# Attention loaded four heads at a time with scores in 32-row tiles, and the second layer of two token runs as seven block products

## The chip, the cores and the metric

One core of one Trainium2 chip. The metric is the device time of one execution in microseconds; the time before is the median of three runs, 688.4 us (688.04 to 689.31). Nothing else runs on the chip.

## What is computed

```python
# attention, for 4 batches x 12 heads x 448 positions x 64 dimensions
scores = np.matmul(q, k.transpose(0, 1, 3, 2)) / np.sqrt(64)
scores = cap * np.tanh(scores / cap)
attn = np.exp(scores - np.max(scores, axis=-1, keepdims=True))
attn = attn / (np.sum(attn, axis=-1, keepdims=True) + 1e-09)
x = np.matmul(attn, v)            # then as 1792 tokens x 768
# multilayer perceptron
h = x @ w_in                      # 768 x 2048, handed in as 64-bit floats
out = np.maximum(0.01 * h, h) @ w_out     # 2048 x 768
```

## The kernel before, in words

**Order of the work.** The program is written as steps (`plan.add`): a rank, the engines that may do it with a cost on each, what it reads and writes, and which old tiles must be free. `Plan.issue` runs a list scheduler over these costs, and emits the instructions in the order that it finds; each engine's order, and which engine a step goes to, are fixed then. The table `T` at the top holds rank offsets of each kind of step, which shift that order.

**Attention.** The 48 heads are 24 pairs (`plan_pair`, line 435). `load_qk` (415) reads the keys or queries of a pair in four transfers of 32 of a head's 64 floats per row; VectorE transposes them in blocks of 32 (line 448), so that a pair lies with its two heads in the upper and lower 64 partitions. Scores are made in four groups of keys: three wide ones of 128 keys for each head as two tiles of 64 rows (499, or 493 where operands are split), and a last one with the 64 keys left of both heads as a block diagonal of 128 rows (496, 490). The first 12 pairs use plain 32-bit matmuls, which show as two records each; later pairs split each operand into a rounded part and a remainder and add three products. ScalarE takes tanh (521) and exp (523) of each group. The groups take turns on two score tiles of two PSUM banks each, `sc`. Values (504) are four groups of two matmuls with 64 columns each, into one of two banks `po`. The sums of the exponentials over keys are added by groups (527, 528, 530) and then, for the first 12 pairs, summed over partitions by a matmul with ones (508) into the other bank `po`, copied and transposed (562). For later pairs (`late_of`, from `tv`) VectorE transposes and reduces them (546, 547) and a small matmul with `fold` (551) adds the parts. A reciprocal, a transpose and a product (581) give the scaled output.

**Layers.** Tokens are cut into four runs: 256, 512, 512 and 512. Run 0 converts each block of weights from 64-bit floats (622 to 629, ScalarE and VectorE), uses it and writes it to a scratch in memory. Run 1 (`plan_unit`, 647) loads these blocks again. From run 1 on every operand is split (`split`, 401: a cast on ScalarE, line 258, and a subtraction on VectorE or GpSimd, line 265) and multiplied as three products of 512 columns. Runs 0 and 1 accumulate in the two banks `m`.

**The last two runs** share their first layer: 2 x 2 blocks of tokens and weights, seven products instead of eight (`plan_blocks`, `plan_duo`, 847; matmuls at 895). Each of the 8 duos leaves four hidden blocks `C` (11, 12, 21, 22; two blocks of hidden features by two runs). `plan_hidden` (950) splits each, and `plan_last` (962) makes the second layer from 18 units of weights (five or six blocks of 128 x 128 each): for each output block and each run 16 blocks x 3 matmuls at line 992, in steps of up to six; then a transpose (1005) and a store (634) in four transfers of 32 columns. The last store is shared by two queues.

## Time and profile before

| | us |
|---|---|
| median of 3 runs | 688.4 |
| profiled execution | 689.4 |
| its span, first to last instruction | 687.6 |
| TensorE busy | 653.6 (95%) |
| VectorE busy | 446.9 (65%) |
| ScalarE busy | 367.7 (53%) |
| GpSimd busy | 73.5 (11%) |
| mean granted TensorE clock | 0.99 |

A stretch's busy time of an engine is the time in which at least one of its instructions ran. A matmul's record lasts longer than the distance to the next, since matmuls are pipelined; the time that one costs is read from how many end in an unbroken stretch. Line 258 and line 265 are helpers that all casts, copies and subtractions share, so their groups are told apart by tile and shape. DMA share is the mean busy share of 16 DMA engines. The clock is given as a share of full speed, 2.4 GHz; the only other level is 1.2 GHz.

### The profile page before, as it was taken

The page shows a single profiled execution, that of the slowest core. Times are in us where ns is not written, and L with a number is a line of the kernel's source. Part 1 is how long each engine was busy: PE and PEld are TensorE (multiplying, and loading weights), DVE is VectorE, ACT ScalarE, POOL GpSimd, SP SyncE. Part 2 cuts the span into 40 slices and gives each one's busy share as a digit, 9 for nine tenths or more (in the row PEclk, how much of TensorE's full clock was granted, in tenths as well). Part 3 has the DMA queues.
Part 4 walks back from the last instruction along what each step waited for, and adds up shares of the span by engine and source line. Part 5 has one row for each costly group of instructions (what it writes and reads, how often), then busy time and mean ns, then how long its engine had stood idle before and what let it go on. Part 6 is the DMA issues. An engine that isn't in the chain of part 4 may idle for free.

```text
span 687.6 us, 8588 instructions
## 1 busy us (share of the span) xinstructions
PE 653.6 (95%) x2932; PEld 457.7 (67%) x2932; DVE 446.9 (65%) x693; ACT 367.7 (53%) x611; POOL 73.5 (11%) x87
## 2 busy tenths in 40 slices
...
GB/s 135 138 237 166 260 246 197 303 256 259 232 130 227 229 170 198 115 46 85 74 91 91 58 95 86 84 47 23 82 33 57 91 42 73 38 92 92 38 27 33
DMA packets 186308, 85.60 MB, mean 124 GB/s; under 512 B 148240, under 2 KB 172816, under 8 KB 186256
## 3 DMA queue, kind: packets, MB, share of 16 engines
...
q0 software_dynamic: 768, 1.38, 1.1%
...
q8 instruction: 25, 0.41, 0.3%
q14 instruction: 27, 0.22, 0.1%
HBM read 66.85 MB, written 18.09 MB: 124 GB/s over the span
## 4 chain that ended last, share of the span: by engine, by line
PE 77%; DVE 8%; ACT 6%; DMA 6%; issue 1%; SPq 1%; DVEq 0%; ACTq 0%
PE m L673 27%; PE sc L992 19%; PE sc L895 11%; PE po L504 7%; PE po L895 4%; PE sc L493 3%; DMA bank<-in_moe_w_in_dram 3%; PE m L895 2%; ACT exps L521 2%; PE sc L499 2%; DVE bank L626 1%; DVE ws L629 1%; ACT exps L523 1%; PE sc L490 1%; DMA scratch<-ws 1%
## 5 line engine op out<-in xcount | busy, mean ns | idle before, releaser
L258 ACT CAST w<-ws 128x384 fp32r<-128x384 f32 (+2 forms) x99 | 62.9, 654 | 133.8 <-PE sc L992 75.1
L265 DVE TENSOR_TENSOR w<-ws,w 128x384 fp32r<-128x384 f32 (+2 forms) x93 | 68.0, 744 | 74.8 <-ACT w L258 74.4
L673 PE MATMUL m<-bank,ws 128*128 128x256 f32 x384 | 92.7, 391 | 2.8 <-DVE ws L629 2.8
L673 PEld LDWEIGHTS m<-bank,ws 128*128 128x128 f32 x384 | 71.7, 192 | 28.6 <-DVE ws L629 8.1
L521 ACT ACTIVATE exps<-sc 128x896 f32<-128x896 f32 (+1 forms) x96 | 76.0, 819 | 27.2 <-PE sc L493 15.1
L504 PE MATMUL po<-exps,norm 128*64 128x448 f32 x384 | 79.5, 547 | 1.3 <-ACT exps L523 0.7
L523 ACT ACTIVATE exps<-exps 128x896 f32<-128x896 f32 (+1 forms) x96 | 79.8, 857 | 0.4
L673 PE MATMUL m<-bank,w 128*128 128x512 f32 x288 | 68.5, 392 | 0.0
L992 PE MATMUL sc<-bank,w 128*128 128x512 f32 x270 | 64.2, 390 | 0.0
L673 PEld LDWEIGHTS m<-bank,w 128*128 128x128 f32 x288 | 53.5, 188 | 12.8 <-issue 1.3
L673 PE MATMUL m<-xh,w 128*128 128x512 f32 x192 | 61.4, 393 | 0.0
L992 PEld LDWEIGHTS sc<-bank,w 128*128 128x128 f32 x270 | 50.7, 188 | 10.9
L504 PEld LDWEIGHTS po<-exps,norm 128*64 128x64 f32 x384 | 25.0, 136 | 45.7 <-issue 36.8
L673 PEld LDWEIGHTS m<-xh,w 128*128 128x128 f32 x192 | 36.0, 188 | 9.7 <-DVE w L265 0.7
L1005 DVE STREAM_TRANSPOSE ot<-sc 128x512 f32<-128x512 f32 x12 | 8.6, 717 | 49.0 <-PE sc L992 49.0
L673 PE MATMUL m<-xl,w 128*128 128x512 f32 x96 | 37.4, 390 | 0.0
L622 ACT ACTIVATE bank<-bank 128x768 int32<-128x768 uint8 (+1 forms) x34 | 29.8, 875 | 12.2 <-DMA bank<-in_moe_w_in_dram 9.9
L626 DVE SCALAR_TENSOR_TENSOR bank<-bank 128x768 int32<-128x768 int32 (+1 forms) x34 | 30.9, 913 | 3.5 <-ACT ws L624 3.4
L527 DVE TENSOR_TENSOR norm<-exps 128x896 f32<-128x896 f32 x23 | 24.9, 1083 | 11.3 <-ACT exps L523 6.6
L629 DVE SCALAR_TENSOR_TENSOR ws<-ws,bank 128x768 int32<-128x768 int32 (+1 forms) x34 | 31.6, 930 | 0.5
L530 POOL TENSOR_TENSOR norm<-norm,exps 64x448 f32<-64x448 f32 x12 | 14.9, 1239 | 154.9 <-ACT exps L523 95.2
L624 ACT ACTIVATE ws<-bank 128x768 f32<-128x768 f32 (+1 forms) x34 | 29.6, 874 | 0.2
(188 smaller groups left out, 1056.2 us busy)
## 6 DMA issues: line engine op xcount, KB each, us to landing
...
```

The costliest lines, as they stand in the source:

```text
L258: nc.scalar.copy(o, i)
L265: ENG[eng].tensor_tensor(out=o, in0=a, in1=f32(b), op=ALU.subtract)
L504: nc.tensor.matmul(at("po", 2 * i)[half[j], 0:S], at("vc", i)[:, c], pf(g)[:, j if wide(g) == 2 else 0], start=(g == 0), stop=(g == NG - 1))
L521: a = plan.add(r, {"act": ct}, lambda e, sc=sc, g=g: nc.scalar.activation(pf(g), sc(), AF.Tanh, scale=scale_of["tanh"]), vers("sc", [g]) + ...
L523: plan.add(r, {"act": ct + 0.03}, lambda e, g=g: nc.scalar.activation(pf(g), pf(g), AF.Exp, scale=scale_of["exp"]), (), vers("pf", [g]), a ...
L622: a = plan.add(rank, {"act": ca}, lambda e: nc.scalar.activation(word(0), top(), AF.Copy, bias=1.0 / 64 - 0.5, scale=1.0 / 32), [("wr", m) ...
L624: b = plan.add(rank, {"act": ca}, lambda e: nc.scalar.activation(ws(), word(1).bitcast(F32), AF.Abs, scale=2.0 ** -112), [("wr", m)], [("w ...
L626: a = plan.add(rank, {"dve": cv}, lambda e: nc.vector.scalar_tensor_tensor(out=word(1), in0=word(1), scalar=-0x80000000, in1=word(0), op0= ...
L629: plan.add(rank, {"dve": cv}, lambda e: nc.vector.scalar_tensor_tensor(out=z(), in0=z(), scalar=3, in1=word(1), op0=ALU.logical_shift_left ...
L673: nc.tensor.matmul(ps(), l, r, start=begins and some[0] == 0 and i == 0, stop=ends and some[-1] == len(cs) - 1 and i == len(ops) - 1)
L895: nc.tensor.matmul(ps(), l, r, start=start and x == 0, stop=x == len(ops) - 1, skip_group_check=not start)
L992: nc.tensor.matmul(ps(), l, rr, start=first and x == 0, stop=final and x == len(ops) - 1)
```

## The change

- A transfer brings the keys or queries of four heads (a quad, two pairs) with 14 neighbouring positions in each partition, 3,584 bytes; tokens therefore stand in another order within a head, and the stores of outputs write them back in theirs, in two pieces where a run crosses a batch (eight transfers instead of four in runs 1 to 3). Values come in eight transfers a pair instead of four.
- A head's 64 dimensions lie as two halves of 32 in the same 32 partitions. A wide group of scores of a quad is four tiles of 32 rows, one a head, two halves added up; it fills all four score banks, one tile `sc` for each pair. The last group is two tiles of 64 rows.
- `late_of` holds from pair 6 instead of 12. For late pairs the last group of values of a quad's two pairs is one step of four tiles of 64 x 64.
- The totals of the first six pairs go to the two banks `m`, instead of sharing `po`.
- The second layer of the last two runs is seven products too. The four hidden blocks of a duo pair are combined and split by `plan_side` (8 for each product, 13 places), the weights by `plan_weights2` (3 pairs of output blocks in two halves for each product, 6 places, 54 loads of 256 KB), `plan_product` multiplies, keeps partial outputs and adds. Its products come in the order 1, 5, 6, 7, 3, 2, 4. `plan_hidden` and `plan_last` go.
- Blocks of w_out are laid in scratch with even hidden blocks first. Six more tiles for exponentials use the place of the split weights until these are needed. All rank offsets in `T` are others.

```diff
-    tv=12,
+    tv=6,
...
-    CHUNKS = [list(range(a, b)) for a, b in ((0, 6), (6, 11), (11, 16))]
+    EVENS_ODDS = [*range(0, NF, 2), *range(1, NF, 2)]
+    CHUNKS = [EVENS_ODDS[a:b] for a, b in ((0, 6), (6, 11), (11, 16))]
...
-    ring("sc", 2, [P, 2, 512], F32, psum)
+    alias("sc", [tile_of(f"sc_{j}", [P, 2, 512], F32, psum) for j in range(2)], [i % 2 for i in range(n_pairs) for _ in range(4)])
     two_banks = [tile_of(f"po_{j}", [P, 512], F32, psum) for j in range(2)]
+    m_banks = [tile_of(f"m_{j}", [P, 512], F32, psum) for j in range(2)]
...
-    alias("po", two_banks, turns(1))
+    alias("po", two_banks + m_banks, [2 * half + i % 2 if i < T["mb"] else turn_ for (i, half), turn_ in zip([(i, half) for i in range(n_pairs) for half in range(2)], turns(1))])
...
+    QUADS = NP // 2
+    part4 = [slice(32 * r, 32 * r + 32) for r in range(4)]
+    def load_qk(src, tag, q_, engine):
+        b, hq = divmod(q_, QUADS)
+        engine.dma_start(out=at(tag, q_), in_=src[b, 4 * hq:4 * hq + 4].rearrange("h s d -> (h s) d").rearrange("(p j) d -> p (j d)", j=NB))
...
+        rows = v[b, 2 * hp:2 * hp + 2].rearrange("h (i j) d -> i h j d", j=NB)
         t = at("vc", i)
-        nc.sync.dma_start(out=t[:, 0:3], in_=rows[:, 0:3])
-        nc.sync.dma_start(out=t[:, 5:8], in_=rows[:, 4:7])
-        for j in range(2):
-            nc.sync.dma_start(out=t[half[j], 3 + j], in_=rows[half[j], 3])
-    def plan_pair(i):
-        plan.part("pair", " zero" if i == 0 else " first" if i < NP else "", i)
-        b, hp = pairs[i]
-        r0 = 10.0 * i
-        if i == 0:
+        for r in range(4):
+            nc.sync.dma_start(out=t[part4[r], :, 0:MID].rearrange("p h c d -> p h (c d)"), in_=rows[:, :, MID * r:MID * r + MID].rearrange("i h j d -> i h (j d)"))
+        for h in range(2):
+            for r in range(2):
+                nc.sync.dma_start(out=t[part4[2 * (h ^ flipped(i)) + r], h, MID], in_=rows[:, h, 4 * MID + r])
...
+        def scores(g):
+            sc = [at("sc", NG * (i0 + j) + g) for j in range(2)]
+            keys = (lambda w: split_of("k", w)) if parted else (lambda w: at("kT", q_))
+            diag = block if parted else (lambda w: at("kb", q_))
+            queries = (lambda w: split_of("q", w)) if parted else (lambda w: at("qT", q_))
+            terms = (("h", "h"), ("h", "l"), ("l", "h")) if parted else (("h", "h"),)
+            ops = [(x, a, c) for x in range(2) for a, c in terms]
+            for n, (x, a, c) in enumerate(ops):
+                flags = dict(start=n == 0, stop=n == len(ops) - 1)
+                if g == MID:
+                    for j in range(2):
+                        nc.tensor.matmul(sc[j][:, 0, 0:S], diag(a)[half[j], x], queries(c)[half[j], x], **flags)
+                else:
+                    for r in range(4):
+                        nc.tensor.matmul(sc[r // 2][:, r % 2, 0:S], keys(a)[part4[r], x, P * g:P * g + P], queries(c)[part4[r], x], **flags)
+        for g in range(NG):
+            if parted:
+                reads = [("kh", q_), ("kw", q_)] if g < MID else [("kp", q_)]
+                reads += [("qh", q_), ("qw", q_)]
+                cost = 6 * MM
+            else:
+                reads = [("kT", q_) if g < MID else ("kb", q_), ("qT", q_)]
+                cost = 2 * BOTH
+            plan.add(r0 + T["pq"] + 5 * g, {"pe": cost}, lambda e, g=g: scores(g), reads, [("sc", NG * (i0 + j) + g) for j in range(2)], mode=1 if g < MID else 3)
...
+        if late_of(i0):
+            plan.part("pair", "", i0)
+            def middle(e):
                 for j in range(2):
-                    part = lambda w=w: at("kh", i) if w == "h" else low("k", i)
-                    plan.add(r0 + T["pk"] + 1, {"dve": 0.15, "act": 0.25}, lambda e, j=j, w=w, part=part: copy(
-                        e, block(w)[half[j], half[j]], f32(part())[half[j], mid_keys[j]]), [("kh", i), ("kw", i), ("fixed_kb", 0)], [("kp", i)])
-        else:
-            for j in range(2):
-                plan.add(r0 + T["pk"] + 1, {"dve": 0.15, "act": 0.25, "pool": 0.5}, lambda e, j=j: copy(
-                    e, at("kb", i)[half[j], half[j]], at("kT", i)[half[j], mid_keys[j]], zeros[half[j]]), [("kT", i)], [("kb", i)])
+                    for i in (i0, i0 + 1):
+                        h = half[j ^ flipped(i)]
+                        nc.tensor.matmul(at("po", 2 * i)[half[j], 0:S], at("vc", i)[h, j, MID], at("pf", NG * i + MID)[h, 0], start=False, stop=True)
+            a = plan.add(r0 + T["pp"] + 17, {"pe": BOTH}, middle, [(t, v_) for i in (i0, i0 + 1) for t, v_ in (("pf", NG * i + MID), ("vc", i))],
+                         [("po", 2 * i0), ("po", 2 * i0 + 2)], mode=4, after=[values_of[i0], values_of[i0 + 1]])
...
-            plan.add(r0 + T["pp"] + 7, {"pe": NG * BOTH}, lambda e: [values(g) for g in range(NG)], vers("pf", range(NG)) + [("vc", i), ("fixed_vx", 0)],
-                     [("po", 2 * i)], mode=2, freed=busy)
+            values_of[i] = plan.add(r0 + T["pp"] + 12, {"pe": MID * BOTH}, lambda e: [values(g) for g in range(MID)], vers("pf", range(MID)) + [("vc", i), ("fixed_vx", 0)],
+                                    [("po", 2 * i)], mode=2, freed=busy)
...
-        lo, hi = RUNS[run]
+        lo, hi = (c // 32 for c in RUNS[run])
+        cuts = [lo] + [c for c in range(0, B * NB + 1, NB) if lo < c < hi] + [hi]
 
         def do(e):
-            for r in range(4):
-                (engines[r] if engines else ENG[e]).dma_start(
-                    out=out[lo:hi, e_ * P + 32 * r:e_ * P + 32 * r + 32].rearrange("(s i) d -> i s d", i=32),
-                    in_=at("ot", o)[32 * r:32 * r + 32, 0:(hi - lo) // 32],
-                )
+            n = 0
+            for c0, c1 in zip(cuts[:-1], cuts[1:]):
+                b, j0 = divmod(c0, NB)
+                rows = out[b * S:b * S + S].rearrange("(i j) d -> i j d", j=NB)[:, j0:j0 + c1 - c0]
+                for r in range(4):
+                    (engines[n % len(engines)] if engines else ENG[e]).dma_start(
+                        out=rows[:, :, e_ * P + 32 * r:e_ * P + 32 * r + 32],
+                        in_=at("ot", o)[32 * r:32 * r + 32, c0 - lo:c1 - lo],
+                    )
+                    n += 1
...
+    SECOND = (1, 5, 6, 7, 3, 2, 4)
+    NK = NF // 2
+    NPQ = NE // 2
+    NSIDE = 13
...
+    def plan_side(idx, n, rank):
+        i = SECOND[idx]
+        blk = lambda b_: (lambda: C_of(n, b_))
+        c = lambda *bs: [("C", c_ver(n, b_)) for b_ in bs]
+        if i == 5:
+            t, src = (blk("12"), blk("11"), c("11", "12"), [made[n, 1]]), blk("11")
+        elif i == 6:
+            t, src = (blk("22"), blk("11"), c("22"), [made[n, 5]]), blk("11")
+        elif i == 7:
+            t, src = (blk("22"), blk("12"), c("12", "22"), [made[n, "T", 5]]), blk("12")
+        elif i == 4:
+            t, src = (blk("21"), blk("11"), c("21"), [made[n, 6]]), blk("11")
+        else:
+            b_ = {1: "11", 3: "22", 2: "21"}[i]
+            t, src, reads = None, blk(b_), c(b_)
+        if t:
+            made[n, "T", i] = tt(rank, src, t[0], t[1], SUB, t[2], [("T", NK * i + n)], after=t[3])
+            reads = [("T", NK * i + n)]
+        k = NK * idx + n
+        if k >= NSIDE:
+            was, n_ = divmod(k - NSIDE, NK)
+            freed = [("p", (was * NPQ + p) * NK + n_) for p in range(NPQ)]
+        else:
+            freed = [gone[2 * k], gone[2 * k + 1]]
+        made[n, i] = split(rank + 0.5, lambda: side(idx, n, "h"), lambda: side(idx, n, "l"), src, W, reads, [("sH", k)], [("sL", k)], freed=freed)
...
+    def plan_weights2(idx, p, hf, rank):
+        i = SECOND[idx]
+        x = 2 * (NPQ * idx + p) + hf
+        s = 2 * p + hf
+        sums = s_home[s][0]
+        if i == 5:
+            load_half(1, 0, p, hf, rank, sums, ("S0", s), s_home[s][1])
+            q_, v_ = load_half(1, 1, p, hf, rank)
+            tt2(rank, sums, sums, q_, ADD, [("S0", s), v_], ("S1", s))
+            src, reads = sums, [("S1", s)]
+        elif i == 6:
+            q_, v_ = load_half(0, 0, p, hf, rank)
+            tt2(rank, sums, sums, q_, SUB, [("S1", s), v_], ("S2", s), after=[s_made[s]])
+            src, reads = sums, [("S2", s)]
+        elif i == 7:
+            q_, v_ = load_half(0, 0, p, hf, rank)
+            q2, v2 = load_half(1, 0, p, hf, rank)
+            tt2(rank, q_, q_, q2, SUB, [v_, v2], ("wz", v_[1]))
+            src, reads = q_, [("wz", v_[1])]
+        elif i == 3:
+            q_, v_ = load_half(0, 1, p, hf, rank)
+            tt2(rank, q_, q_, sums, SUB, [v_, ("S2", s)], ("wz", v_[1]))
+            src, reads = q_, [("wz", v_[1])]
+        else:
+            q_, v_ = load_half(*{1: (0, 0), 2: (0, 1), 4: (1, 1)}[i], p, hf, rank)
+            src, reads = q_, [v_]
+        slot = x % NW2
...
+        bk = {1: a_banks[p], 6: a_banks[p], 7: a_banks[p], 4: a_banks[p], 5: b_banks[p], 3: b_banks[p], 2: d_banks[p % 2]}[i]
+        ps = lambda: bank(*bk)
+        start = i in (1, 5, 2)
+        ip = NPQ * idx + p
+        n_duos = NF // 2
+        if i == 1:
+            freed, after = [("a4", k) for k in range(n_duos - 3, n_duos) if a_banks[k % 3] == bk], []
+        elif i == 5:
+            freed, after = [("b2", k) for k in range(n_duos - 3, n_duos) if b_banks[k % 3] == bk], []
+        elif i == 2:
+            freed, after = ([("r", ip - 2)] if p == 2 else [("d", k) for k in range(n_duos - 2, n_duos) if d_banks[k % 2] == bk]), []
+        else:
+            freed, after = [], [copied[{6: 1, 7: 6, 4: 7, 3: 5}[i], p]]
+        prev = []
+        for n0 in range(0, NK, 2):
+            def mm(e, n0=n0):
+                ops = []
+                for n in (n0, n0 + 1):
+                    u = w_half2(2 * ip + n // 4)
+                    hi, lo = (u[:, a, P * (n % 4):P * (n % 4) + P] for a in range(2))
+                    ops += [(hi, side(idx, n, "h")), (hi, side(idx, n, "l")), (lo, side(idx, n, "h"))]
+                for x, (l, r) in enumerate(ops):
+                    nc.tensor.matmul(ps(), l, r, start=start and n0 == 0 and x == 0, stop=n0 == NK - 2 and x == len(ops) - 1, skip_group_check=not start)
+            prev = [plan.add(rank + 0.68 * n0, {"pe": 6 * MMW}, mm,
+                             [("uh", 2 * ip + n0 // 4), ("ul", 2 * ip + n0 // 4)] + [(t, NK * idx + n0 + k) for k in range(2) for t in ("sH", "sL")],
+                             [("p", NK * ip + n0), ("p", NK * ip + n0 + 1)] + ([("r", ip)] if n0 == NK - 2 else []), after=prev or after, freed=freed if not prev else ())]
+        r = rank + 5
+        b_ = {1: "11", 5: "22", 6: "12", 7: "22", 3: "12", 2: "11", 4: "21"}[i]
+        row, run = int(b_[0]) - 1, 1 + int(b_[1])
+        o = 2 * NE + ip - 3 * NPQ
+        if i in (1, 5, 6):
+            y, yf = y_home[b_, p]
+            copied[i, p] = plan.add(r, {"act": act(W), "dve": 0.07 + 1.04e-3 * W}, lambda e: copy(e, y(), ps()), [("r", ip)], [("y", NPQ * int(b_) + p)], port=False, freed=yf)
+            return
...
+        if i == 4:
+            src, reads = ps, [("r", ip)]
+        else:
+            src = y_home[b_, p][0]
+            copied[i, p] = plan.add(r, {"dve": 0.07 + 1.04e-3 * W}, lambda e: nc.vector.tensor_tensor(out=src(), in0=ps(), in1=src(), op=ADD),
+                                    [("r", ip), ("y", NPQ * int(b_) + p)], [("yz", NPQ * int(b_) + p)], port=False)
+            reads = [("yz", NPQ * int(b_) + p)]
+        plan.add(r, {"dve": turn(W)}, lambda e: nc.vector.transpose(out=at("ot", o).rearrange("p s d -> p (s d)"), in_=src()), reads, [("ot", o)], port=False)
+        cost, engines = {"sp": 4.2}, None
+        if i == 4 and p == NPQ - 1:
+            cost, engines = {"sp": 2.1}, [nc.sync, nc.scalar]
+        plan.add(r + 1, cost, store(o, run, 2 * p + row, engines), [("ot", o)], (), xfer=1.8, port=False)
...
+    def plan_second(rank):
+        for idx in range(len(SECOND)):
+            for n in range(NK):
+                plan.part("side", "", NK * idx + n)
+                plan_side(idx, n, rank + 3 * 24 * MMW * idx - T["sd"] + 1.5 * n)
+            for p in range(NPQ):
+                plan_product(idx, p, rank + 24 * MMW * (NPQ * idx + p))
```

## Rows read from the trace of the kernel before

**Rows 1.** Busy time by stretch (us): each engine, then clock, DMA share, GB/s.

```profile
0.00:60.00 60.00, 48.36 (x184) 18.30 (x184) 34.80 (x64) 46.51 (x71) 21.51 (x40) 0.94 0.92 174
60.00:117.00 57.00, 54.28 (x234) 29.14 (x234) 43.43 (x67) 41.99 (x66) 7.11 (x9) 0.97 0.87 219
117.00:195.00 78.00, 76.37 (x364) 47.57 (x361) 66.31 (x105) 64.95 (x106) 6.53 (x9) 1.00 0.95 251
195.00:235.00 40.00, 35.68 (x188) 22.95 (x187) 36.90 (x56) 33.61 (x57) 6.08 (x6) 1.00 0.83 210
235.00:420.00 185.00, 184.75 (x876) 135.49 (x877) 142.54 (x207) 106.02 (x176) 21.10 (x15) 1.00 0.41 106
420.00:545.00 125.00, 120.95 (x518) 96.40 (x517) 86.03 (x147) 54.03 (x106) 11.17 (x9) 1.00 0.20 58
545.00:680.00 135.00, 133.22 (x578) 107.82 (x576) 36.51 (x54) 20.63 (x32) 0.00 (x0) 1.00 0.26 56
```

**Rows 2.** Chain of waits in order of time: start us, us, what.

```profile
30.51 8.58 DMA bank<-in_moe_w_in_dram
...
578.07 101.59 PE sc L992 x441
```

**Rows 3.** Groups of VectorE by form: busy us, mean ns, idle before.

```profile
L265 DVE TENSOR_TENSOR bank<-xh,bank 128x512 fp32r<-128x512 f32 x6 | 4.1, 685 | 0.0
...
L909 DVE SCALAR_TENSOR_TENSOR bank<-bank 128x512 f32<-128x512 f32 x18 | 12.5, 692 | 0.2
...
L546 DVE STREAM_TRANSPOSE norm<-norm 128x896 f32<-128x896 f32 x12 | 13.3, 1107 | 0.8 <-POOL norm L530 0.4
...
L547 DVE TENSOR_REDUCE rs<-norm 128x28 f32<-128x896 f32 x12 | 12.9, 1079 | 0.2
...
L562 DVE STREAM_TRANSPOSE norm<-norm 128x448 f32<-128x448 f32 x12 | 7.8, 648 | 2.2 <-ACT norm L258 2.2
```

**Rows 4.** Groups of ScalarE by form, same columns.

```profile
L523 ACT ACTIVATE exps<-exps 128x896 f32<-128x896 f32 x72 | 67.4, 950 | 0.3
L521 ACT ACTIVATE exps<-sc 128x896 f32<-128x896 f32 x72 | 64.6, 913 | 25.8 <-PE sc L493 15.1 <-PE po L504 7.0 <-PE sc L499 3.3
...
L258 ACT CAST bank<-wait 128x512 fp32r<-128x512 f32 x6 | 3.7, 623 | 4.8 <-DVE bank L265 3.5 <-PE m L673 1.3
```

**Rows 5.** Timeline, GpSimd and VectorE side by side: start us, us, what.

```profile
543.20 1.30 POOL L265 TENSOR_TENSOR odd<-bank,odd 128x512 fp32r<-128x512 f32 x1 [0.55 <-ACT odd L258]
543.25 1.80 DVE L909 SCALAR_TENSOR_TENSOR xh<-xh 128x512 f32<-128x512 f32 x1
```

**Rows 6.** Timeline of TensorE, values and plain scores: start us, us, what, records.

```profile
32.81 3.23 PE L504 MATMUL po<-exps,norm 128*64 128x448 f32 x16 [0.58 <-DVE norm L581]
...
88.68 1.77 PE L499 MATMUL sc<-norm 64*128 64x448 f32 x8
```

**Rows 7.** Chain of waits, 340 to 360 us, scores in three terms.

```profile
345.15 1.44 PE sc L493 x12
...
349.75 0.80 PE sc L493 x6
```

**Rows 8.** Groups of TensorE by form: values, totals by ones, totals by fold.

```profile
L504 PE MATMUL po<-exps,norm 128*64 128x448 f32 x384 | 79.5, 547 | 1.3 <-ACT exps L523 0.7 <-DVE norm L581 0.6
...
L508 PE MATMUL po<-norm,ones 128*64 128x448 f32 x48 | 13.5, 589 | 0.4 <-DVE norm L530 0.4
...
L551 PE MATMUL po<-rs,fold 128*128 128x28 f32 x24 | 3.9, 244 | 0.2 <-DVE xh L581 0.2
```

**Rows 9.** DMA packets, from the page.

```profile
DMA packets 186308, 85.60 MB, mean 124 GB/s; under 512 B 148240, under 2 KB 172816, under 8 KB 186256
```

**Rows 10.** Timeline, first transposes and last stores: start us, us, what.

```profile
5.74 1.17 DVE L448 STREAM_TRANSPOSE norm<-raws 128x448 f32<-128x448 f32 x2 [4.10 <-DMA raws<-in_k_dram]
...
679.69 0.72 DVE L1005 STREAM_TRANSPOSE ot<-sc 128x512 f32<-128x512 f32 x1 [10.32 <-PE sc L992]
680.44 1.82 SPq L639 DMA_DIRECT2D out_dram<-ot  x2
```

403 lines of the change are left out of this document (209 added, 194 removed).

## The prediction, made before the change was run

> **What bounds the kernel now.** I first read the busy time by stretch [rows 1]. TensorE is busy 653.6 of 688 us, and from 235 us on it hardly pauses: 184.8 of 185 us in the first-layer run of 512 tokens, 121.0 of 125 in the block products of the first layer, 133.2 of 135 in the second layer of the last two runs. Before 235 us it loses 11.6, 2.7, 1.6 and 4.3 us to idling, and the clock granted is 0.94 and 0.97 of full speed in the first two stretches (part of them ran at 1.2 instead of 2.4 GHz) and 1.00 after. There the other engines are nearly as full: ScalarE 46.5 of 60 us, VectorE 66.3 of 78 and then 36.9 of 40, the DMA engines 0.83 to 0.95. In the last 135 us VectorE has only 36.5 us of work and ScalarE 20.6: that is the room which the change uses. Second, the chain of waits [rows 2]: it ends in 101.6 us of unbroken second-layer matmuls, 441 of them, so 0.2304 us each; early it runs through single transfers such as 8.6 us for one block of w_in. So a matmul removed after 235 us is time removed, if the other engines keep up; before 235 us only part of it is.
>
> The profiled execution took 689.4 us (span 687.6 and 1.8 around it), 1.0 above the median of 688.4. I sum against 689.4 and take 1.0 off at the end.
>
> **The second layer, matmuls.** Before, 16 x 6 block pairs x 2 runs x 3 terms = 576 matmuls of 512 columns. After, 7 products x 3 output pairs x 8 x 3 terms = 504. 72 x 0.2304 = **-16.6 us**, all on the path.
>
> **The second layer, the other engines.** New are 56 splits of hidden blocks with 32 sums, and 42 splits of weight halves with 24 sums. A split is a cast on ScalarE and a subtraction on VectorE, a sum one VectorE operation, all 128x512 [rows 3]. VectorE: (56 + 42 + 32 + 24) x 0.685 = 105 us, and some 21 evictions and transposes at about the same price, 14: together 120 us beside 504 x 0.2304 = 116 us of TensorE. ScalarE: 98 casts and 9 copies x 0.623 = 67 us [rows 4], which the matmuls hide. VectorE isn't hidden everywhere. The order of products is 1, 5, 6, 7, 3, 2, 4. Each of 5, 6 and 7 needs 8 x 2 + 6 x 2 = 28 operations, 19.2 us, while a product of three pairs lasts 72 x 0.2304 = 16.6 us: 2.6 us late three times, at most 7.8. Operands of the first product can be made during the last first-layer duo, and the 13 slots for hidden blocks and 6 for weights let the late ones trail by part of a product. Lower bound 0, upper 7.8; I take the middle, **+4**. Product 3 (20 operations) and 2 (14) give it no way back to TensorE. GpSimd, offered every sum and subtraction, is no relief: a leak of 128x512 takes VectorE 0.692 us in the mean [rows 3], and one that ran beside a subtraction of 1.3 us on GpSimd took 1.8 [rows 5], so what GpSimd takes over VectorE loses again. The 54 loads of 256 KB in place of 18 of 320 to 384 KB fall where DMA is busy 0.26 [rows 1] and lead by 15 us: nothing.
>
> The first layer's duos lose the 32 hidden splits that lay among them, 22 us of VectorE in a stretch where TensorE idles 4.0 us: **-1.5** (0 to -3).
>
> **Scores.** Each pair's 64-row tiles become, for a quad, two accumulated 32-row parts in four tiles, so twice the matmuls. What a quad's wide group costs depends on how many tiles run at once. Rows show two at a time: 12 matmuls of split scores with 448 columns take 1.44 us [rows 7], 0.12 each, where one of 512 columns alone takes 0.2304 [rows 2]; two groups of plain ones, 8 records, take 1.77 [rows 6]. If four run at once, a quad's group takes what two pair groups take now. If two, a plain one takes as long as 16 records do, 3.23 [rows 6], 1.46 more, and a split one 2 x 1.44 less one start of 0.17, 1.27 more; with 18 of each 26 + 23 = 49 us. Bounds 0 and +49; I take **0**, because 64-row tiles lose nothing against each other, which is the nearest row, and keep the other end as a rival. The Trainium skill (TensorEngine Tiling (Array Packing), Overview, Theoretical Speedup) gives a factor of up to 4 for contractions of at most 32, by which the price would be 0 as well; no trace here shows four.
>
> The steps of scores halve, 96 to 48. Two split steps in one go take 1.44, apart 2 x 0.80 [rows 7], so a start saved is worth some 0.17: 48 x 0.17 = 8. Some already follow each other: **-6** (0 to -9).
>
> **Values and totals.** From pair 6 on the middle group of a quad is four 64x64 tiles in one step. A group costs 79.5 / 96 = 0.83 us [rows 8], two 1.66; four tiles at once should cost one group, 0.9 with its own start: 9 quads x 0.75 = **-6.7** (0 if only two run together). Pairs 6 to 11 drop the matmul with ones (13.5 / 12 = 1.13) for the fold (3.9 / 12 = 0.33) [rows 8]: **-4.8**.
> In exchange VectorE gets, for each of the six, 1.11 + 1.08 - 0.65 = 1.54 us, 9.2 in all [rows 3], between 60 and 195 us, where it has 25 us of idle time [rows 1], but is waited for: **+3** (0 to 9.2).
>
> **Loads, start, banks.** Keys and queries come as 128-byte pieces now, 24 x 2 x 2 x 896 = 86,016 of the page's 148,240 packets under 512 B [rows 9]; after, as 3,072 of 3.5 KB. That takes load from a DMA share of 0.87 to 0.95. It can return at most the idle time before 117 us less the 6.9 until the first operands are transposed [rows 10], 14.3 - 6.9, and the lost clock, 60 x 0.06 + 57 x 0.03 = 5 us: 12; the pairs are then also bounded by ScalarE, so **-4** (0 to -12). The totals of the first six pairs in the two MLP banks, empty until run 0, are part of this. SyncE has fewer issues for keys and queries but 8 instead of 4 for values and for outputs of the last three runs; off the path but for the end: 4 instead of 2 stores on each of two queues, which took 1.82 for 2 [rows 10], part of it under the landing: **+1.5** (0 to 2). The first scores wait for four transposes instead of two (1.17 for two [rows 10]): **+1**.
>
> **Sum.** -16.6 + 4 - 1.5 - 6 - 6.7 - 4.8 + 3 - 4 + 1.5 + 1 = -30.1. 689.4 - 30.1 - 1.0 = **658 us**.
>
> **Rivals.**
> *VectorE sets the pace.* The late operands cost the full 7.8 (+3.8), the six pairs' totals their full 9.2 (+6.2), and the DMA relief returns nothing (+4): 672; without the saved steps 678. For it: VectorE at 36.9 of 40 us before 235 and 120 us of work beside 116. Against it: the slack of slots. 0.22.
> *The transfers were the brake early.* The full 12 of relief (-8), no late operands (-4), 9 of steps (-3): 643. For it the 8.6 us piece [rows 2]; against it ScalarE's load. 0.12.
> *Score banks.* A quad's group fills all four score banks, so the next must wait for both tanh; two tanh and two exp take 2 x 0.913 + 2 x 0.950 = 3.7 us [rows 4], and the next scores have only the exps' 1.9 us to run their 1.77. Whatever step TensorE has in front then idles ScalarE, half of a 1.6 us step on average: in the first three quads 12 groups x 0.8 = +10, 668. The Trainium skill (TensorEngine Tiling (Array Packing), Gotcha 1: PSUM Pressure) says that row tiling raises the pressure on PSUM since tiles need banks of their own; no trace here shows it. 0.10.
> *Four tiles run two at a time: slower.* Place: the 36 wide score groups. Price 49, of which the first three quads (13) may fall into idle time: 694 to 707, say 705. It turns the sign once more than 30 of the 49 us are real, that is below about 2.5 tiles at once. 0.08.
> *The change doesn't do what it says*: the products reuse sums in place, and a wait that I haven't seen, of operand on operand, leaves TensorE idle as long as it is spared: 688. 0.02.
> The forecast keeps 0.46.
>
> **Numbers.** A measurement can tell about 0.2%, 1.4 us, from nothing. The forecast and the first three rivals are faster, 0.90; I move 0.03 of it to the other sides for prices that may all be short: faster 0.87, same 0.03, slower 0.10. The range reaches from the second rival to beyond the first, 643 to 680, and leaves out the slower one and the unchanged.
>
> **What would show it.** Second layer: 504 matmuls at 0.2304 us; idle time before them named VectorE, about 4 us in the products 5, 6 and 7. Quad groups of plain scores of about 1.8 us and of split ones of 1.4; twice that means the slower rival. Middle steps of 0.9 us. A DMA share well under 0.9 before 195 us. Granted clock nearer 1.00 before 117. Wrong I'd be if TensorE idles over 15 us in the second layer, if its idle time before 235 us grows, or if ScalarE's idle time behind scores (rows of tanh) rises by over 10 us.

## The result and the profile after

The changed kernel takes **659.55 us** (median of 4 runs, 658.96 to 660.13) against 688.22 us of the kernel before on the same chip (4 runs, 686.73 to 689.31): ratio 0.9585, 95% interval 0.9564 to 0.9605. Faster by 28.7 us; forecast were 658 us and a range of 643 to 680. The profiled execution took 659.37 us, its span 657.6 (before 689.4 and 687.6).

The page of the kernel after, first the busy times with their share of the span, then the DMA packets:

```profile
PE 625.3 (95%) x3268; PEld 445.1 (68%) x3268; DVE 504.4 (77%) x801; ACT 394.2 (60%) x644; POOL 112.3 (17%) x98
...
DMA packets 106729, 93.52 MB, mean 142 GB/s; under 512 B 55217, under 2 KB 85937, under 8 KB 106673
```

ScalarE's tanh on the scores by form after (line 573; in 24 of the 96 the output lies in `w`), first on the wide groups, then on the last ones; below it the last groups before, which [rows 4] leaves out:

```profile
L573 ACT ACTIVATE exps<-sc 128x896 f32<-128x896 f32 x56 | 50.4, 921 | 21.8 <-PE sc L517 14.5 <-DVE norm L582 3.2 <-PE po L563 1.8
...
L573 ACT ACTIVATE w<-sc 128x896 f32<-128x896 f32 x16 | 14.6, 926 | 3.1 <-PE sc L517 3.0
...
L573 ACT ACTIVATE exps<-sc 128x448 f32<-128x448 f32 x16 | 8.3, 549 | 8.4 <-PE sc L514 8.4
```

```profile
L521 ACT ACTIVATE exps<-sc 128x448 f32<-128x448 f32 x24 | 12.9, 538 | 1.4 <-PE po L504 1.3
```

ScalarE idles before the wide groups' tanh 24.9 us (25.8 before), before the last groups' 8.9 (1.4 before; the eight in `w`, not shown, have 0.5).

Busy time by stretch after, with the columns of [rows 1] and its stretches but the last:

```profile
0.00:60.00 60.00, 51.67 (x288) 21.74 (x292) 36.00 (x73) 52.11 (x81) 10.74 (x24) 1.00 0.68 212
60.00:117.00 57.00, 56.00 (x316) 33.23 (x308) 49.66 (x80) 46.99 (x73) 17.49 (x15) 1.00 0.72 224
117.00:195.00 78.00, 72.39 (x398) 49.66 (x396) 65.79 (x102) 55.32 (x81) 9.22 (x9) 0.96 0.82 259
195.00:235.00 40.00, 39.59 (x279) 25.72 (x278) 37.63 (x59) 31.10 (x51) 10.63 (x7) 1.00 0.70 210
235.00:420.00 185.00, 184.32 (x1037) 134.42 (x1030) 138.14 (x205) 111.01 (x178) 39.34 (x26) 1.00 0.34 91
420.00:545.00 125.00, 121.14 (x528) 98.32 (x527) 99.26 (x167) 52.74 (x103) 17.94 (x14) 1.00 0.31 90
545.00:657.60 112.60, 100.20 (x440) 81.98 (x438) 77.91 (x122) 44.96 (x81) 6.94 (x5) 0.96 0.44 101
```

Against [rows 1]: up to 117 us TensorE idles 9.3 us and not 14.4, and the granted clock is 1.00 where it was 0.94 and 0.97 (60 x 0.06 + 57 x 0.03 = 5.3 us given back). From 117 to 195 us it is the other way: 5.6 us idle where 1.6 were, and the clock at 0.96 (3.1 us lost). From 195 to 235 idle goes from 4.3 to 0.4. In the last stretch VectorE is at 77.9 of 112.6 us where it had 36.5 of 135, and TensorE still runs through until its last matmul.

Four heads in 32-row tiles, in the timeline of TensorE after (start us, us, line, names, tile, count): a plain wide group of a quad, its last group, a split wide group, a middle step of values.

```profile
121.72 1.79 PE L517 MATMUL sc<-heads 32*128 32x448 f32 x16
126.22 1.77 PE L514 MATMUL sc<-heads 64*128 64x448 f32 x8
347.50 1.49 PE L517 MATMUL sc<-heads 32*128 32x448 f32 x24
334.98 0.98 PE L538 MATMUL po<-exps,norm 64*64 64x448 f32 x8
```

16 records in 1.79 us, where 8 of 64 rows took 1.77 [rows 6], and 24 in 1.49, where 12 took 1.44 [rows 7]: four tiles run at once. The Trainium skill (TensorEngine Tiling (Array Packing), Overview, Theoretical Speedup) gives a speedup of up to 4 for a small dimension of at most 32; these rows, 16 records where there were 8 and 24 where there were 12, agree.

### The profile page after: what moved, and what is told of

It is laid out like the page before. It is cut to its first block, busy times and chain, and to the rows that moved or that the text cites. A ratio compares the mean times of both kernels' runs of the same rounds, so it can differ in the third digit from the quotient of the medians.

```text
span 657.6 us, 9482 instructions
## 1 busy us (share of the span) xinstructions
PE 625.3 (95%) x3268; PEld 445.1 (68%) x3268; DVE 504.4 (77%) x801; ACT 394.2 (60%) x644; POOL 112.3 (17%) x98
## 4 chain that ended last, share of the span: by engine, by line
PE 71%; DVE 8%; DMA 8%; ACT 5%; SPq 4%; issue 2%; DVEq 0%; ACTq 0%
PE m L755 29%; PE sc L980 10%; PE sc L517 7%; PE po L563 6%; PE sc L1163 5%; PE po L980 4%; DMA bank<-in_moe_w_out_dram 3%; PE m L980 2%; SPq L720 2%; PE po L1163 2%; PE sc L514 2%; PE m L1163 2%; DVE w L273 2%; DMA ws<-scratch 1%; DMA scratch<-ws 1%
## 5 line engine op out<-in xcount | busy, mean ns | idle before, releaser
L266 ACT CAST w<-ws 128x384 fp32r<-128x384 f32 (+3 forms) x98 | 60.4, 627 | 66.7 <-PE m L755 18.2
L755 PEld LDWEIGHTS m<-bank,ws 128*128 128x128 f32 x384 | 71.8, 193 | 24.8 <-DVE ws L704 5.1
L273 DVE TENSOR_TENSOR w<-ws,w 128x384 fp32r<-128x384 f32 (+3 forms) x90 | 66.5, 750 | 21.0 <-ACT w L266 20.3
L573 ACT ACTIVATE exps<-sc 128x896 f32<-128x896 f32 (+1 forms) x72 | 58.7, 838 | 30.3 <-PE sc L517 14.5
L517 PE MATMUL sc<-heads 32*128 32x448 f32 x720 | 63.1, 457 | 5.0 <-DVE heads L475 1.4
L755 PE MATMUL m<-xh,w 128*128 128x512 f32 x192 | 63.9, 400 | 0.4 <-DVE w L273 0.3
L576 ACT ACTIVATE exps<-exps 128x896 f32<-128x896 f32 (+1 forms) x72 | 61.4, 873 | 0.6
L517 PEld LDWEIGHTS sc<-heads 32*128 32x128 f32 x720 | 34.4, 187 | 31.0 <-issue 10.0
L563 PE MATMUL po<-exps,norm 128*64 128x448 f32 x232 | 49.0, 549 | 0.7 <-ACT exps L576 0.4
L563 PEld LDWEIGHTS po<-exps,norm 128*64 128x64 f32 x232 | 14.7, 136 | 27.1 <-issue 21.5
L584 POOL TENSOR_TENSOR norm<-norm,exps 64x448 f32<-64x448 f32 x13 | 15.4, 1188 | 72.4 <-DVE norm L582 44.5
L980 PE MATMUL sc<-exps,w 128*128 128x512 f32 x90 | 24.8, 395 | 2.3 <-ACT bank L266 1.4
L1163 PE MATMUL sc<-exps,w 128*128 128x512 f32 x102 | 26.5, 389 | 0.0
```

Source lines behind the costliest of these rows:

```text
L266: nc.scalar.copy(o, i)
L273: ENG[eng].tensor_tensor(out=o, in0=a, in1=f32(b), op=ALU.subtract)
L517: nc.tensor.matmul(sc[r // 2][:, r % 2, 0:S], keys(a)[part4[r], x, P * g:P * g + P], queries(c)[part4[r], x], **flags)
L563: nc.tensor.matmul(at("po", 2 * i)[half[j], 0:S], at("vc", i)[:, j, g], pf(g)[:, j if wide(g) == 2 else 0], start=(g == 0), stop=(g == NG ...
L573: a = plan.add(r, {"act": ct}, lambda e, sc=sc, g=g: nc.scalar.activation(pf(g), sc(), AF.Tanh, scale=scale_of["tanh"]), vers("sc", [g]) + ...
L576: plan.add(r + 2, {"act": ct + 0.03}, lambda e, g=g: nc.scalar.activation(pf(g), pf(g), AF.Exp, scale=scale_of["exp"]), (), vers("pf", [g] ...
```

## The experiments

Each is compared with 659.55 us by its median; the ratio is to the kernel before in the same runs (there 687.2 to 688.9 us). All changes are to the kernel after, but for e2; e12 starts from e9. The runs were made on four chips, on which the kernel before differs by up to 1.7 us, so a difference of 2 us or less between two kernels that did not run side by side is not told from nothing.

**Where the tiles lie (e1, e2).** The 512-column products turned out faster one by one, [rows 2] giving 101.59 / 441 = 230.4 ns apiece. Chain of waits after, in pieces of such products alone:

```profile
383.53 17.79 PE m L755 x78
...
612.89 12.25 PE m L1163 x54
```

The second is 226.9 ns apiece. The change allocates the small tiles of the reciprocals ahead of the chunk tiles, no longer behind them, which shifts what lies between by 128 bytes. In the kernel before, that shift set the chunks apart from w, xl, xh and the banks; after, all lie alike; with the small tiles at their old place in the changed kernel (e1), the chunks and w lie apart from xl, xh and the banks.

e1:
```diff
-    ring("rt", 2, [P, NB, 1])
     rows = chunk("raws", ("kraw", 1, 2 * S, None), ("qraw", 1, 2 * S, None))
...
     fold = const.tile([P, P], F32, name="fold")
+    ring("rt", 2, [P, NB, 1])
```

> The changed kernel with the two small tiles of the reciprocals placed in SBUF behind the chunk tiles again, as the kernel before has them; no instruction is added or moved. The 512-column products were 229.8 to 231.5 ns apart before and 226.95 after, by the tile that is streamed. Theory A (the streamed tile and the weight tile should lie alike modulo 256 bytes): here the chunk tiles and w lie at 32, xl, xh and the banks at 160, so products that stream xl, xh or a bank go to about 232 ns and those that stream a chunk tile stay at 227. Theory B (only the streamed tile's own place counts, 32 is slow): the chunk tiles go to about 232, xl, xh and banks stay at 227. Theory C (the spacing has to do with something else that the change did): all stay at 227. A or B: 661 to 664 us, C: 659.5.

Measured: 662.62 us, ratio 0.9631 [0.9606, 0.9656]. Chain of waits of e1, the same 78 products of run 1, which stream a bank:

```profile
386.28 18.21 PE m L755 x78
```

18.21 - 17.79 is 5.4 ns apiece. The timeline of the second layer, first after, then e1, same instructions:

```profile
565.33 2.20 PE L1163 MATMUL po<-xl,w 128*128 128x512 f32 x9
...
568.73 1.52 PE L1163 MATMUL sc<-exps,w 128*128 128x512 f32 x6
```

```profile
569.74 2.26 PE L1163 MATMUL po<-xl,w 128*128 128x512 f32 x9
...
573.22 1.52 PE L1163 MATMUL sc<-exps,w 128*128 128x512 f32 x6
```

What streams xl or a bank became slower, what streams a chunk (exps) did not: theory A. Theory B would have slowed the chunks. In the kernel before it was the other way round, by the starts of its matmuls: 232 ns from chunk tiles, 227 to 229 from banks and xl.

e2, the kernel before:
```diff
+    ring("rt", 2, [P, NB, 1])
     rows = chunk("raws", ("kraw", T["raw"], S, by32), ("qraw", T["raw"], S, by32))
...
     fold = const.tile([P, P], F32, name="fold")
-    ring("rt", 2, [P, NB, 1])
```

> The kernel before with the two small tiles of the reciprocals moved ahead of the chunk tiles, as the change does, and nothing else. If their place is what sets the spacing of the 512-column products (theories A and B), all of them come to about 227 ns (L895 231.5, L992 229.8 before) and the time falls by 3 to 5 us, to 683.5 to 685.5. If not (theory C), 688 us and the spacing as it was.

Measured: 684.01 us, ratio 0.994 [0.9917, 0.9963], so -4.8 against 688.85 by the medians and -4.1 by the ratio. Its chain, beside [rows 2]:

```profile
573.24 100.28 PE sc L992 x441
```

101.59 has become 100.28 (227.4 ns apiece). A tile's place alone is worth 3 to 5 us in either kernel; e1 slows other matmuls (xl, xh, banks) than e2 speeds up (the chunks). That it is the distance modulo 256 bytes was tried with this one shift only.

**The end (e3).**
```diff
-        if i == 4 and p == NPQ - 1:
+        if i == 4:
             cost, engines = {"sp": 2.1}, [nc.sync, nc.scalar]
```

> The changed kernel with the stores of the last three output tiles issued by two queues by turns (SyncE and ScalarE) where the change has only the last one so. Theory A (the end waits for SyncE to issue 8 transfers a tile): 2 to 4 us less, 655.5 to 657.5, last matmul to end 8 to 10 us where it took 12.1. Theory B (the transposes and the landing set the end): 659.5, unchanged within 1.

Measured: 655.89 us, ratio 0.9538 [0.9512, 0.9563]. The view of the stores' line (issues, count: ns min/median/max, first and last start in us), first after, then e3:

```profile
L720 SPq DMA_DIRECT2D out_dram<-ot x39: 315/436/1802, 629.7 to 652.3; - x39
...
L720 ACTq DMA_DIRECT2D out_dram<-ot x4: 425/462/717, 647.9 to 649.6; - x4
```

```profile
L720 SPq DMA_DIRECT2D out_dram<-ot x27: 315/433/1551, 629.8 to 647.3; - x27
L720 ACTq DMA_DIRECT2D out_dram<-ot x12: 323/453/1454, 635.7 to 647.2; - x12
```

The last matmuls in the timeline, after and e3:

```profile
644.69 0.84 PE L1163 MATMUL po<-raws,w 128*128 128x512 f32 x3
```

```profile
642.66 0.84 PE L1163 MATMUL po<-raws,w 128*128 128x512 f32 x3
```

From the end of the last matmul to the end of the span: 657.6 - 645.5 = 12.1 us after, 652.6 - 643.5 = 9.1 here. Theory A, 3 of the 3.7 us; the other 2 us of the profiled execution lie ahead of it, in code that is the same. The stores hold up the last tile too: its transpose after,

```profile
647.15 0.72 DVE L1183 STREAM_TRANSPOSE ot<-po 128x512 f32<-128x512 f32 x1 [4.59 <-DMA out_dram<-ot]
```

waits until an earlier tile has been stored, 1.6 us past the last matmul; in e3 it starts at 643.54, 0.04 past it.

**SyncE's queue in the heads (e4, e5, e8, e9).** In the chain of waits after, 130 to 175 us is mostly transfers; between these pieces lie SyncE's issues of value loads (L445, L448):

```profile
132.26 7.43 DMA bank<-in_moe_w_out_dram
...
140.89 5.82 DMA scratch<-ws
...
148.04 4.88 DMA bank<-in_moe_w_out_dram
...
156.89 7.27 DMA bank<-in_moe_w_out_dram
...
170.69 2.48 DMA scratch<-ws
```

e4 moves the value loads to POOL:
```diff
-            nc.sync.dma_start(out=t[part4[r], :, 0:MID].rearrange("p h c d -> p h (c d)"), in_=rows[:, :, MID * r:MID * r + MID].rearrange("i h j d -> i h (j d)"))
+            ENG[e].dma_start(out=t[part4[r], :, 0:MID].rearrange("p h c d -> p h (c d)"), in_=rows[:, :, MID * r:MID * r + MID].rearrange("i h j d -> i h (j d)"))
...
-        plan.add(r0 - T["al"] + 1, {"sp": 4.2}, lambda e: load_v(i), [("fixed_vx", 0)], [("vc", i)], xfer=0.9)
+        plan.add(r0 - T["al"] + 1, {"sp": 4.2} if i < 2 else {"pool": 4.2}, lambda e: load_v(i, e), [("fixed_vx", 0)], [("vc", i)], xfer=0.9)
```

> The changed kernel with the value loads of all pairs but the first two (eight transfers a pair) issued by POOL and not SyncE; the planner orders the rest anew by its own costs. Theory A (SyncE's queue, filled with value loads from 130 to 175 us, holds the second layer's weight loads and the scratch stores back): TensorE idles 3 to 4 us less from 130 to 195 us and keeps its full clock there, 652 to 656 us. Theory B (the transfers themselves are late, the DMA share being 0.82 there, whatever queue issues them): 659.5 or, with POOL's subtractions late, 661 to 664.

Measured: 705.72 us, ratio 1.024 [1.0214, 1.0266]. A miss: POOL's groups show

```profile
L445 POOL DMA_DIRECT2D norm<-in_v_dram x88 | 47.2, 542 | 63.8 <-PE po L563 58.9 <-PE po L538 2.4 <-DMA norm<-in_v_dram 2.4
```

POOL stands waiting until the values' buffer is free, with its sums and subtractions behind that wait, and the planner orders everything anew. It tells nothing of SyncE.

e5 (order unchanged):
```diff
-                nc.sync.dma_start(out=t[part4[2 * (h ^ flipped(i)) + r], h, MID], in_=rows[:, h, 4 * MID + r])
+                [nc.sync.dma_start(out=t[part4[2 * (h ^ flipped(i)) + r], h, MID], in_=rows[:, h, 4 * MID + r]) for _ in range(2 if i >= 2 else 1)]
```

> The changed kernel with the four small value transfers (8 KB each) of every pair but the first two issued twice by SyncE, in the same place; no other instruction is added or moved. Four more issues of some 0.6 us a pair, 88 in all, and few bytes. Theory A (SyncE's queue holds the second layer's loads and the scratch stores back between 130 and 195 us): the 7 or so pairs whose loads lie there add 2.4 us each to SyncE's queue and TensorE idles 5 to 15 us longer there: 665 to 675. Theory B (issue time on SyncE is hidden): 659 to 661.

Measured: 768.48 us, ratio 1.1164 [1.1131, 1.1197], far beyond either theory. SyncE's waits say why:

```profile
SPq L448 <- DMA norm<-in_v_dram: 132.3, 88, 3.9
```

Each repeated transfer waits until the first one to its place has landed, 1.5 us in the mean. The waits are semaphore instructions of the program (114 at line 448, where after has 31), so the edit added more than issues. So SyncE was held up by 132 us and 88 issues of some 0.32 us, some 160 in all, and 109 of that reached the end. The queue has little slack; but the values themselves came late too, so this sets no price for eight issues against four.

e8 moves the loads of w_out and the stores of the converted tiles to POOL:
```diff
-                nc.sync.dma_start(out=at("wr", m)[:, lo:lo + len(fs)], in_=src[:, fs[0]:fs[-1] + 1:2])
+                nc.gpsimd.dma_start(out=at("wr", m)[:, lo:lo + len(fs)], in_=src[:, fs[0]:fs[-1] + 1:2])
...
-        plan.add(rank - T["wd"], {"sp": 1.2 if units[m][0] == "l2" and units[m][1] == 1 else 0.6}, lambda e: w_raw(m), (), [("wr", m)], xfer=0.46 * n)
+        plan.add(rank - T["wd"], {"pool": 1.2 if units[m][1] == 1 else 0.6} if units[m][0] == "l2" else {"sp": 0.6}, lambda e: w_raw(m), (), [("wr", m)], xfer=0.46 * n)
...
-        plan.add(rank + 2, {"sp": 0.6}, lambda e: nc.sync.dma_start(out=scratch[m], in_=ws()), [("ws", m)], [(f"scratch{m}", 0)], xfer=0.23 * n)
+        plan.add(rank + 2, {"pool" if units[m][0] == "l2" else "sp": 0.6}, lambda e: ENG[e].dma_start(out=scratch[m], in_=ws()), [("ws", m)], [(f"scratch{m}", 0)], xfer=0.23 * n)
```

> The changed kernel with the loads of w_out and the stores of the converted w_out issued by POOL and not SyncE (34 transfers); the planner orders the rest anew. Theory A (SyncE's queue is what makes them late, e5): idle between 130 and 195 us falls from 5.6 to 2 or less with the clock at 1.00, 653 to 656. Theory B (the transfers are slow by themselves): 659 to 661. Theory C (POOL's order makes it worse, as with the value loads): over 665.

Measured: 698.33 us, ratio 1.0158 [1.0126, 1.019]. Theory C, with a new order of the planner as in e4: inconclusive for SyncE.

e9 keeps the order and the bytes, and issues half as often:
```diff
-        for r in range(4):
-            nc.sync.dma_start(out=t[part4[r], :, 0:MID].rearrange("p h c d -> p h (c d)"), in_=rows[:, :, MID * r:MID * r + MID].rearrange("i h j d -> i h (j d)"))
+        for h in range(2):
+            nc.sync.dma_start(out=t[:, h, 0:MID].rearrange("p c d -> p (c d)"), in_=rows[:, h, 0:4 * MID].rearrange("i (r c) d -> r i (c d)", r=4))
         for h in range(2):
-            for r in range(2):
-                nc.sync.dma_start(out=t[part4[2 * (h ^ flipped(i)) + r], h, MID], in_=rows[:, h, 4 * MID + r])
+            nc.sync.dma_start(out=t[half[h ^ flipped(i)], h, MID], in_=rows[:, h, 4 * MID:4 * MID + 2].rearrange("i r d -> r i d"))
```

> The changed kernel with the values of a pair loaded by four transfers (two of 128 partitions x 192, two of 64 x 64) in place of eight; the same bytes, and the order on every engine as it was. 96 issues of some 0.45 us fewer on SyncE. Theory A (SyncE's queue holds the loads of w_out and the scratch stores back from 130 to 195 us): idle of TensorE there falls from 5.6 us to 2 or less, the half clock of 6.8 us goes, 652 to 656. Theory B (the transfers themselves are slow, and what SyncE's queue costs was made by e5's own waits): 658.5 to 660.

Measured: 656.39 us, ratio 0.9537 [0.9514, 0.9559], -3.2. Busy time in the two stretches between 130 and 175 us where TensorE idles, first after, then e9:

```profile
130.00:145.00 15.00, 14.01 (x72) 8.62 (x70) 14.15 (x25) 9.58 (x16) 6.55 (x4) 1.00 0.74 214
...
160.00:175.00 15.00, 11.31 (x66) 8.49 (x64) 13.66 (x25) 9.64 (x17) 2.10 (x2) 0.98 0.70 210
```

```profile
130.00:145.00 15.00, 13.96 (x71) 8.72 (x70) 14.07 (x26) 9.89 (x16) 6.50 (x4) 1.00 0.83 262
...
160.00:175.00 15.00, 10.64 (x63) 8.27 (x63) 12.57 (x23) 10.58 (x20) 2.69 (x2) 0.98 0.62 183
```

The time lies just above theory A's 652 to 656, the place is not A's: the idle time stayed (5.4 us from 130 to 195, where after has 5.6). The loads of w_out and the scratch stores left the chain of waits, and the next work, which ends almost as late, took their place (chain of e9):

```profile
131.16 1.01 DVE bank L701
...
133.82 1.02 DVE norm L605
...
135.26 1.09 DVE rs L606
...
165.09 0.72 DVE bank L701
```

These are VectorE's conversions of w_out and its part in the late totals. Where e9's 3 us lie is not settled: its last matmul ends 2.0 us earlier than after's and the tail is 0.9 shorter, but the clock from 160 to 195 us also differs where the code is the same (0.98 and 0.84 after, 1.00 and 0.91 in e3).

**The totals on VectorE (e12, on e9).**
```diff
-    flat = lambda t: t.rearrange("p j s -> p (j s)")
+    flat, cut = lambda t: t.rearrange("p j s -> p (j s)"), lambda i: P if 8 <= i < 12 else 2 * S
...
-            plan.add(rt_, {"dve": 1.04}, lambda e: nc.vector.transpose(out=flat(at("tT", i)), in_=flat(at("t", i))), [("t", i)], [("tT", i)], port=False)
+            plan.add(rt_, {"dve": 1.04}, lambda e: nc.vector.transpose(out=flat(at("tT", i))[:, 0:cut(i)], in_=flat(at("t", i))[:, 0:cut(i)]), [("t", i)], [("tT", i)], port=False)
...
-                out=flat(at("rs", i)), in_=flat(at("tT", i)).rearrange("p (b k) -> p b k", k=32), op=ALU.add, axis=mybir.AxisListType.X),
+                out=flat(at("rs", i))[:, 0:cut(i) // 32], in_=flat(at("tT", i))[:, 0:cut(i)].rearrange("p (b k) -> p b k", k=32), op=ALU.add, axis=mybir.AxisListType.X),
```

> e9's kernel in which VectorE's transpose and sum for the totals of pairs 8 to 11 cover 128 of the 896 columns (the other columns' totals of these pairs are left out); the order on every engine is e9's. It takes some 1.9 us from VectorE four times, at 107, 120, 135 and 146 us. With the value loads halved, e9's chain between 130 and 138 us runs through these operations and the conversions of w_out on VectorE. Theory A (the totals that moved to VectorE are what delays the conversions, the prediction's +3): idle between 130 and 195 us falls from 5.4 to 2 us or less, and 652.5 to 654.5. Theory B (the delay lies in the conversions' own order, after 146 us): 655.5 to 656.5, idle 4.5 or more.

Measured: 653.82 us, ratio 0.951 [0.9492, 0.9529]: 2.6 less than e9 by the medians, 1.9 by the ratios (the interval overlaps e9's). Busy time by stretch of e12:

```profile
130.00:145.00 15.00, 15.00 (x76) 9.72 (x77) 13.77 (x27) 10.64 (x18) 6.55 (x4) 1.00 0.80 262
...
160.00:175.00 15.00, 11.62 (x63) 8.96 (x62) 13.53 (x25) 11.08 (x18) 2.01 (x2) 0.92 0.67 202
```

Between the theories: the idle time of 130 to 145 us (1.0) is gone, that of 160 to 175 fell from 4.4 to 3.4 us. From 130 to 195 us 2.0 us went, and the last matmul ends 2.1 us earlier (641.4 for 643.5). So the first came from the totals; the second waits for conversions whose chain runs through VectorE and ScalarE, with transposes of a later quad's keys in it (162 to 172 us), and what would shorten it was not tried. The edit takes away whole totals (1.9 us a pair), more than what moved to VectorE (1.5).

**The packets (e6).**
```diff
-        engine.dma_start(out=at(tag, q_), in_=src[b, 4 * hq:4 * hq + 4].rearrange("h s d -> (h s) d").rearrange("(p j) d -> p (j d)", j=NB))
+        rows_ = src[b, 4 * hq:4 * hq + 4].rearrange("h s d -> (h s) d").rearrange("(p j) (x d) -> p x j d", j=NB, x=2)
+        for x in range(2):
+            engine.dma_start(out=at(tag, q_).rearrange("p (j x d) -> p x j d", x=2, d=32)[:, x], in_=rows_[:, x])
```

> The changed kernel with each load of keys and queries as two transfers in pieces of 128 bytes, as the kernel before has them (the same bytes, some 83,000 packets more, 24 issues more). Theory A (the packets were the brake before 117 us, as the prediction's term of -4 to -12 has it): idle before 117 us rises from 9.3 towards the 14.4 of before, half clock comes back, 664 to 671. Theory B (ScalarE and VectorE set the pace there): 660 to 662, the rest being SyncE's extra issues.

Measured: 684.32 us, ratio 0.9944 [0.9926, 0.9962]. Busy time by stretch of e6:

```profile
0.00:60.00 60.00, 46.95 (x240) 19.34 (x240) 24.25 (x51) 40.50 (x61) 7.89 (x20) 0.89 0.91 183
60.00:117.00 57.00, 50.21 (x277) 25.71 (x276) 45.73 (x78) 45.97 (x72) 15.81 (x15) 0.94 0.86 161
117.00:195.00 78.00, 72.55 (x375) 49.69 (x374) 69.51 (x110) 55.12 (x84) 14.07 (x11) 0.97 0.84 262
195.00:235.00 40.00, 36.22 (x242) 24.74 (x241) 28.26 (x42) 29.08 (x43) 5.06 (x3) 0.89 0.98 218
```

Theory A, and three times its size: with the small pieces 24.8 of the 28.7 us are gone. Idle before 235 us is 29.1 us for 15.4, and the lost clock (60 x 0.11 + 57 x 0.06 + 78 x 0.03 + 40 x 0.11) 16.8 for 3.1. The large pieces are what the rest of the change in the heads stands on. Packets and the 24 more issues on SyncE were not told apart by a run of their own; 96 issues fewer gave 3.2 us (e9), so 24 more are an unlikely cause of most of it.

**Sums in the MLP banks (e7).**
```diff
-    mb=6,
+    mb=0,
```

> The changed kernel with the totals of the first six pairs kept in the two attention banks by turns and not in the MLP banks, so that a pair's totals share the banks with values. Theory A (the banks saved a wait): values of the first quads wait for evictions, TensorE idles 3 to 6 us more before 60 us: 662 to 666. Theory B (that stretch hangs on ScalarE's tanh and exp): 659 to 661.

Measured: 708.83 us, ratio 1.029 [1.0258, 1.0322]. Before 60 us TensorE is busy 47.6 us for 51.67, as theory A has it, but the planner's order differs from there on and most of the 49 us lie after 117 us. What the banks are worth by themselves stays open.

**VectorE in the second layer (e11).**
```diff
-        ENG[eng].tensor_tensor(out=o, in0=a, in1=f32(b), op=ALU.subtract)
+        [ENG[eng].tensor_tensor(out=o, in0=a, in1=f32(b), op=ALU.subtract) for _ in range(times)]
...
-        return plan.add(rank, {e: cl[e] for e in lo_eng}, lambda e: sub(e, o_lo(), src(), o_hi()), reads, lo, after=[a, *after], freed=freed)
+        return plan.add(rank, {e: cl[e] for e in lo_eng}, lambda e: sub(e, o_lo(), src(), o_hi(), times if e == "dve" else 1), reads, lo, after=[a, *after], freed=freed)
...
-        made[n, i] = split(rank + 0.5, lambda: side(idx, n, "h"), lambda: side(idx, n, "l"), src, W, reads, [("sH", k)], [("sL", k)], freed=freed)
+        made[n, i] = split(rank + 0.5, lambda: side(idx, n, "h"), lambda: side(idx, n, "l"), src, W, reads, [("sH", k)], [("sL", k)], freed=freed, times=2 if i in (5, 6, 7) else 1)
```

> The changed kernel with the subtraction that makes the low part of a hidden block done twice in VectorE's products 5, 6 and 7 (up to 24 more of 0.69 us, 16.5 us of VectorE, no other order). VectorE has 5.5 us of idle time within those three products, 2.2 and 4.2 us in the next two. Theory A (the low end of the prediction's term: VectorE is ahead of TensorE there and its lead and idle time take the load): 659 to 662. Theory B (VectorE is just at its limit, the term is 0 by a hair): what exceeds the 5.5 us comes out at the end, 668 to 673.

Measured: 673.68 us, ratio 0.9788 [0.9766, 0.981], +14.1. Busy time by stretch from about the start of product 5 on, after and then e11:

```profile
543.50:560.30 16.80, 16.66 (x73) 13.46 (x73) 15.94 (x27) 9.51 (x18) 0.00 (x0) 1.00 0.41 123
560.30:577.30 17.00, 17.00 (x76) 14.06 (x75) 15.23 (x26) 7.82 (x16) 0.00 (x0) 1.00 0.41 102
577.30:594.50 17.20, 17.20 (x77) 14.24 (x77) 14.29 (x23) 9.91 (x19) 2.66 (x2) 1.00 0.38 115
```

```profile
543.50:562.00 18.50, 16.43 (x71) 12.98 (x70) 17.41 (x29) 9.03 (x17) 0.00 (x0) 1.00 0.40 126
562.00:581.00 19.00, 14.93 (x59) 11.78 (x58) 18.76 (x31) 8.73 (x16) 0.00 (x0) 0.91 0.21 55
581.00:600.00 19.00, 16.85 (x67) 13.41 (x66) 16.11 (x27) 6.16 (x11) 0.00 (x0) 0.91 0.42 117
```

Counted by 72 matmuls a product, product 5 lasts 16.8 us after and 25.0 here, product 6 16.3 and 20.4, product 7 16.3 in both. Theory B, and a little more: VectorE does 23 more subtractions, 23 x 0.69 - 5.5 = 10.4 us, and the clock at 0.91 over 38 us costs another 3.4. The change meets its price on VectorE without loss, but with nothing to spare.

**A version that beats both (e10):** e9 and e3 together.

> e9 and e3 together: values of a pair in four transfers, and the last three output tiles stored by SyncE and ScalarE by turns. If theory A holds in both, the two gains lie at different ends of the kernel and add: 649 to 652.5. If only e3's holds: 655 to 656.5.

Measured: **655.0 us**, ratio 0.9512 [0.9486, 0.9538], below the interval of the change. Whether the two gains add is open: 659.55 - 3.7 - 3.2 would be 652.7, the lowest of the five runs (652.66 to 655.94). The tail is 9.8 us (12.1 after, 9.1 in e3), and 0.9 of e9's gain was tail as well, which the stores shorten anyway.

## Why the prediction came out right

The sum was -30.1, the span fell by 30.0, in good part by errors that cancel: that the direction and the largest term held is no luck, that the number came so near is. For TensorE's own time I sum, line by line, from a matmul's start to the next one's, idle time left out.

| term | forecast | measured |
|---|---|---|
| second-layer matmuls | -16.6 | -17.8 (133.3 to 115.5 us) |
| late operands of VectorE | +4 | 0: TensorE 100.2 of 100.5 us from 545 us to its last matmul |
| duos' idle | -1.5 | idle 4.0 to 3.9; their matmuls -2.1 |
| score steps | -6 | -0.8 |
| middle values | -6.7 | -5.5 |
| totals on TensorE | -4.8 | -5.5 |
| loads and banks | -4 (to -12) | before 117 us -5.0 idle, -5.3 clock |
| totals on VectorE | +3 (to 9.2) | 117 to 195 us: +4.0 idle, +3.1 clock; e12: some 2 of it |
| tail | +1.5 (to 2) | +4.1 (8.0 to 12.1) |
| first scores | +1 | +0.8 (they start at 6.96 and 7.80 us) |

The clock shares stand twice, in the rows of the loads and of the totals on VectorE and in the matmuls that ran at the lower clock, so the column has no sum.

**Right.** The matmuls removed after 235 us are time removed: 72 x 0.2304. The four tiles at once (0, not +49) and the middle steps. The score banks cost nothing where that rival put its +10: before the first 24 tanh, those of three quads, ScalarE idles 1.8 us in all where it was 4.4; over the kernel it idles 33.8 where it was 27.2, less than the rival's sign of 10 more, and behind the wide scores (line 517) 17.5 where it was 18.4 [rows 4]. The Trainium skill (TensorEngine Tiling (Array Packing), Gotcha 1: PSUM Pressure) says that row tiling raises the pressure on PSUM; these rows show no price of it. The totals on VectorE at +3 fit e12, which finds some 2 us for four of the six pairs, on e9's kernel and with overlapping intervals; the size is not shown. None of the signs of being wrong came: TensorE idles 0.3 us in the second layer up to its last matmul, and 15.4 before 235 us where it was 20.3.

**Wrong step 1, "take the middle, +4" for VectorE's late operands.** It cost nothing. The sum counted 28 operations a product, 19.2 us against 16.6, three times; the rows show VectorE busy 15.9, 15.2 and 14.3 us there, with 27, 26 and 23 operations, evictions among them. So some of the 28 ran ahead of their product; that the 13 slots allowed it is argued, as no run took slots away. e11 shows the margin: the lower bound held by a hair.

**Wrong step 2, the scores' -6.** Starts were saved only where two steps stood apart: 2 x 0.80 became 1.49, but pairs that followed each other already (1.44) had nothing to give, and a quad's plain group still takes 1.79.

**Wrong step 3, the tail's "part of it under the landing".** Not only the last tile pays for eight transfers: the tiles before it fill SyncE's queue (its last store starts at 652.3 us) and hold the last transpose back by 1.6 us. e3 returns 3 us of the 4.1.

**Missed, the place of the tiles.** The forecast kept 230.4 ns a matmul. 1008 matmuls in the block products and the second layer were 3 to 5 ns quicker: some 4 us (e2, the same shift in the kernel before, -4.1 to -4.8), which made up for most of the scores.

**The loads**, the term most mis-sized, came in near their outer bound: -10.3 and not -4, if all that changed before 117 us is put to them (the share of the banks is open, e7). e6 shows the large pieces to be the condition of nearly all the gain. The rival that made the transfers the brake had the relief and the absent late operands right, and 9 us of steps wrong. "Off the path" for SyncE's eight value transfers was wrong by at most e9's 3.2 us; what I first read from the chain, that they cause the idle time of 130 to 195 us, fell with e9. Of the 7.1 us lost between 117 and 195 us (4.0 idle, 3.1 clock) some 2 are traced to the totals; the rest is open.
